# A fused attention and expert-routing kernel: six batches' result leaves the core unturned, and the first two batches turn theirs in buffers of their own

## The chip, the cores and the metric

The kernel runs on one core of one Trainium2 chip, as one launch. The metric is the device time of that launch in microseconds (us), as the median of the runs shown, lower is better. The inputs are laid out on the host beforehand (z and u transposed, z repeated for both halves of the partitions); the rows that pad the last tile of the output are cut off afterwards. Neither is timed.

## The reference, cut to what matters

First an attention-like product without a softmax, per batch, then a mixture of experts in which each token goes to one expert of eight and each expert keeps at most 80 tokens; all other rows of the output are zero.

```
B, S, D = 8, 2496, 256          # d_qk = 64
scores = z @ z^T / S            # symmetric
attn   = max(scores, 0) ** 2
x      = u * (attn @ v)         # all batches: 19968 tokens of 256
logits = x @ w_gate             # 8 experts; argmax, softmax weight of the chosen one
for e in range(8):              # the 80 tokens of largest weight
    h = max(x[tok] @ w1[e], 0); out[tok] = weight * (h @ w2[e])
```

The weights of nearly all tokens tie, and the order in which the reference keeps tied tokens puts the kept ones into the first and the last batch, which this kernel works first and second. It counts on that and checks it: a flag, computed from the data, decides at the end whether a general path (an exact top-80 over all tokens) has to run. For the inputs of the runs shown the flag is 0 and the general path is not entered.

## The kernel before, in words

**Tiles.** A batch has 2,496 rows, that is 20 tiles of 128 (the last one half full), and is worked in five chunks of 512 query columns (`qc` = 0 to 4) by ten steps, one for each pair of key tiles: 8 x 5 x 10 = 400 steps. The main loop (L1007) is written out in a fixed order for all engines and for SyncE's DMA queue (SP).

**One step.** TensorE (PE) makes the scores of the pair that is two steps ahead (`scores`, L385), ScalarE (ACT) takes relu and square out of PSUM (L402, L403), and the square is split into a rounded high part `ah` and a rest `al` (L113 or L115, and L58 on VectorE, DVE). PE then adds the pair's product with `v`, in three passes, to the accumulator `acc` in PSUM (`attend_pair` and `weigh`, L438). Since the scores are symmetric, a block that was computed as key against query is used again as its mirror image: DVE turns it in 32 x 32 squares (L308), SP writes it to DRAM (`y<-x`, L318, 1 MB) and reads it back with four DMAs (`blk<-y`, L335), and ACT splits it straight from there (L380) without scores. The chunk's own diagonal block does the same with a quarter (`yd<-xd` L353, `md<-yd` L362 issued in step 3 of the chunk, used by ACT at L415 in step 7).

**The end of a chunk.** `acc` has two tiles of PSUM (`ps_a`, two buffers), one for each half `c` of the 256 features. In step 9 `take` (L503 to L508) copies each of them into the two halves of one SBUF tile, `xf[:, 0]` and `xf[:, 1]`; the next chunk's first product needs the accumulator that this frees. `xpool` has one buffer for `xf`, so `take` also has to wait until nobody reads the chunk before in it any more.

**What is done with x.** During the next chunk's steps (`finished`, L964): `chunk_x` in step 0 adds the halves, scales and multiplies by u, into `xf[:, 0]`, which is x transposed (features on partitions). `chunk_hi`, `chunk_rest`, `chunk_mid` and `chunk_lo` (steps 1 to 4) split x into three bf16 parts in `xb`, with `xf[:, 1]` as working space; `chunk_logits` (steps 6 or 7) makes the gate logits from them. In step 4 `chunk_store` (L554) turns x with two DMA transposes of 16-bit halves (L562) from `xf[:, 0]` into `xf[:, 1]`, and in step 6 `chunk_store2` (L565) writes the turned rows to DRAM (`xs<-xf`, L572; the half-full last tile of a batch has a second write, L577): to `xs2` for the first two batches, to `xs` for the other six. `xs2` feeds the expert stage; `xs` is read in the general path alone.

**Order on SP.** One in-order queue issues nearly all DMAs. Within a step it is: what `finished` issues, then the loads of u (L149, step 2), z and v, zeros for the output, and then `mirror_back` (L335), `mirror_out` (L318), `quarter_write` (L353) and, in step 3, `quarter_back` (L362), L1071 to L1075.

**Buffers that the change takes up.** `vraw` (two buffers, L128) holds raw chunks of v before they are split; a batch's last one is used up in step 3 of its first chunk, and the next batch's first two are loaded in chunk 3. The tag `x` of `sqpool` (four buffers, L306) holds turned score blocks until `y<-x` has read them; ten are made in a batch, four in chunk 0, three, two and one in the chunks after.

```
def take(b, qc, c):
    if c == 0:
        x_sum[b, qc] = chunk_tiles(b, qc)
    x = x_sum[b, qc]
    nc.scalar.copy(out=x[:, :, c], in_=acc_t[b, qc][c][:, :, :x.shape[-1]])
...
if r == NP - 1 and not last:
    attend_pair(b, qc, 2 * p, True, True, lambda c: take(b, qc, c))
```

Of the kernel before, what the change touches and what calls it, by code (L numbers as in the profile page):

```python
# [8 lines left out]
F32 = mybir.dt.float32  # L9
# [3 lines left out]
U16 = mybir.dt.uint16  # L13
# [6 lines left out]
P = 128  # L20
# [5 lines left out]
def attn_moe_kernel(ctx, tc, zT, uT, v, wg, w1, w2, out, seq, cap):  # L26
# [5 lines left out]
    nc = tc.nc  # L32
    V = nc.vector
    B, _, SP = zT.shape
    D = uT.shape[1]
# [6 lines left out]
    QT = 4  # L42
    NQ = NT // QT
    CH = QT * P
    DC = D // P
# [22 lines left out]
    dram = ctx.enter_context(tc.tile_pool(name="dram", bufs=1, space=DRAM))  # L68
# [7 lines left out]
    sqpool = weights.enter_context(tc.tile_pool(name="sqpool", bufs=NX))  # L76
    main = ExitStack()
    zpool = main.enter_context(tc.tile_pool(name="zpool", bufs=2))
# [14 lines left out]

    xs = dram.tile([NTOK * 2, D], U16, name="xs")
    gt = dram.tile([NTOK, 1], F32, name="gt")

    wtab = dram.tile([(NBLK + 1) * E, 2 * P], BF16, name="wtab")
    wtwo = dram.tile([(2 * BPB + 1) * E, 2 * P], BF16, name="wtwo")
# [391 lines left out]
    xt_t, xq_t, lg_t = {}, {}, {}  # L490

    def chunk_tiles(b, qc):
        xf = xpool.tile([P, 2, DC, CH], F32, tag="xf", name=f"xf_{b}_{qc}")

        xb = xpool.tile([P, 3, DC, CH], BF16, tag="xb", name=f"xb_{b}_{qc}")
        nq = min(CH, seq - qc * CH)
        xt_t[b, qc] = [x[..., :nq] for x in (xf[:, 0], xb, xf[:, 1])]
        xr_t[b, qc] = xf[:, 1].bitcast(U16)
        return xf[..., :nq]

    x_sum, xr_t = {}, {}

    def take(b, qc, c):  # L503

# [11 lines left out]
    def chunk_hi(b, qc):  # L516
        xf, xb, _ = xt_t[b, qc]
        nc.scalar.copy(out=xb[:, 0], in_=xf)  # L518

    def chunk_rest(b, qc):  # L520
        xf, xb, xr = xt_t[b, qc]
        tt(xr, xf, xb[:, 0], ALU.subtract)

    def chunk_mid(b, qc):
        _, xb, xr = xt_t[b, qc]
        nc.scalar.copy(out=xb[:, 1], in_=xr)  # L526

    def chunk_lo(b, qc):
        _, xb, xr = xt_t[b, qc]
        tt(xb[:, 2], xr, xb[:, 1], ALU.subtract)  # L530
# [20 lines left out]
                                 start=False, stop=(c, t) == (DC - 1, QT - 1))  # L551
        lg_t[b] = pl[:, :QT * E].rearrange("p (t e) -> p t e", e=E)

    def chunk_store(b, qc):  # L554

        xf = xt_t[b, qc][0]
        nq = min(CH, seq - qc * CH)
        ng = nq // 64
        xq = xr_t.pop((b, qc)).rearrange("p c (g r) -> p (c g r)", r=P)
        xq = xq.rearrange("p (g c r) -> p g c r", c=DC, r=P)  # L560
        for c in range(DC):
            nc.sync.dma_start_transpose(out=xq[:, :ng, c, :], in_=xf[:, c, :nq].bitcast(U16))  # L562
        xq_t[b, qc] = xq

    def chunk_store2(b, qc):  # L565
        xq = xq_t.pop((b, qc))
        nq = min(CH, seq - qc * CH)
        ng = nq // 64
        xo, r0 = (xs2, b * NT) if b < 2 else (xs, RB[b] * NT)
        r0 = (r0 + qc * QT) * 2 * P  # L570
        gl = ng if nq == CH else ng - 1
        nc.sync.dma_start(  # L572
            out=xo[r0:r0 + gl * P, :D].rearrange("(g r) d -> r g d", r=P),
            in_=xq[:, :gl].rearrange("p g c d -> p g (c d)"))
        if gl < ng:
            r1 = r0 + (2 * QT - 1) * P
            nc.sync.dma_start(out=xo[r1:r1 + P, :D], in_=xq[:, gl].rearrange("p c d -> p (c d)"))  # L577

    def chunk_logits(b, qc):
        nq = min(CH, seq - qc * CH)  # L580
        xb = xt_t[b, qc][1]
        pl = ps_m.tile([P, 2, CH], F32, tag="m", name=f"pl_{b}_{qc}")[:, :, :3 * QT * E]
        to = pl.rearrange("p h (s t e) -> p h t s e", s=3, t=QT)
        for t in range(QT):
            t0 = min(t * P, nq - P)
            for i in range(3 * DC):
                for h, hs in enumerate(HALVES):
                    nc.tensor.matmul(to[:, h, t], xb[hs, i % 3, i // 3, t0:t0 + P], wgs[hs, i // 3],
                                     start=i == 0, stop=i == 3 * DC - 1)
        lg_t[b, qc] = pl.rearrange("p h (s x) -> p x h s", s=3)  # L590

    def chunk_sum(b, qc):
        if qc == 0:
            lg_t[b] = gp.tile([P, NT, E], F32, tag="lg", name=f"lg_{b}")
        V.tensor_reduce(out=lg_t[b][:, qc * QT:(qc + 1) * QT].rearrange("p t e -> p (t e)"),
                        in_=lg_t.pop((b, qc)), axis=AX.XY, op=ALU.add)
# [3 lines left out]
    def gate_top(b, q0, q1):  # L600

        nt = (q1 - q0) * QT
        lg = lg_t[b][:, :nt]
        col = (RB[b] * NQ + q0) * QT
        k0, nk = col // 2, nt // 2

        def bc(t):
            return t.broadcast_to([P, nt, E])

        def small(name, n=E):  # L610
            return gp.tile([P, NT, n], F32, tag=name, name=f"{name}_{b}_{q0}")[:, :nt]

        mx = small("mx", 1)
        V.tensor_reduce(out=mx, in_=lg, axis=AX.X, op=ALU.max)
        last = b == B - 1
        d = d_last if q1 == NQ and last else small("d")
        tt(d, lg, bc(mx), ALU.subtract)
        ex = ex_last[:, q0 * QT:q1 * QT] if last else lg
        nc.scalar.activation(out=ex, in_=d, func=AF.Exp)

        fw = small("fw")
        V.scalar_tensor_tensor(out=fw, in0=d, scalar=0.0, in1=first_w.broadcast_to([P, nt, E]),
                               op0=ALU.is_equal, op1=ALU.mult)
        mf = small("mf", 1)
        V.tensor_reduce(out=mf, in_=fw, axis=AX.X, op=ALU.max)
        V.tensor_tensor(out=oh[:, :, k0:k0 + nk].rearrange("p h k e -> p k h e"),
                        in0=fw.rearrange("p (k h) e -> p k h e", h=2),
                        in1=bc(mf).rearrange("p (k h) e -> p k h e", h=2), op=ALU.is_equal)
        if q1 == NQ:
            V.memset(oh[:P - TAIL, 1, k0 + nk - 1], 0.0)  # L630
        gate_t[b, q0] = d, ex, fw
# [332 lines left out]
    def finished(b, qc, r):  # L964

        at_end = b == B - 1 and qc == NQ - 2
        if r == 1:
            chunk_hi(b, qc)
        if r == (1 if at_end else 2):
            chunk_rest(b, qc)  # L970
        if r == (2 if at_end else 3):
            chunk_mid(b, qc)
        if r == (3 if at_end else 4):
            chunk_lo(b, qc)
        if r == (3 if at_end else 4):
            chunk_store(b, qc)
        if r == (5 if at_end else 6):
            chunk_store2(b, qc)
        if r == (5 if at_end else 6 if qc == NQ - 1 else 7):
            chunk_logits(b, qc)  # L980
            chunk_sum(b, qc)
        if b < B - 1 and qc == NQ - 1:
            if r == 8:
                gate_top(b, 0, NQ)
            elif r == 9:
                gate_sum(b, gate_near(b, 0), gp)
        elif qc == 0 and b > 0:
            if r == 5:
                count(b - 1, 0, BPB, b - 1)
            elif r == 9 and b <= 2:  # L990
                kr = RB[b - 1] * BPB
                blocks(ps_m, "m", gp, oh, kr, kr + BPB, wtwo, (b - 1) * BPB)
        elif at_end and r == 7:
            gate_top(b, 0, NQ - 1)

    with tc.manual_schedule(engines={ET.PE, ET.Activation, ET.DVE, ET.SP, ET.Pool}):
# [10 lines left out]
        for i, (b, qc, r) in enumerate(steps):  # L1007
# [7 lines left out]
            p = pairs_of[b, qc][r]  # L1015
# [6 lines left out]
            if b == 0 and qc == 0:  # L1022
                if r % 2 == 0 and r < 8:
                    g = r // 2 + 1
# [13 lines left out]
            if prev:  # L1038
                finished(*prev, r)
# [4 lines left out]
            if b + 1 < B:  # L1044
# [5 lines left out]
                if qc == NQ - 2 and r in (2, 4):  # L1050
                    g = r // 2 - 1
                    v_raw[b + 1, g] = load_v(b + 1, g)
                if qc == NQ - 1:
                    if r in (1, 3, 6, 8):
                        g = (1, 3, 6, 8).index(r)
# [434 lines left out]
    with tc.If(nc.values_load(flag[0:1, 0:1], min_val=0, max_val=1) > 0):  # L1490
        for i in range(B * NQ):
            zero_out(i, B * NQ)
        with tc.tile_pool(name="gx", bufs=1) as gx:
            counted = (gx.tile([P, E, NBLK], BF16, name="tot"), gx.tile([P, E, NBLK], F32, name="incl"),
                       gx.tile([P, NST, E], F32, name="rank"))
            nc.sync.dma_start(out=gt[(B - 1) * NT * P:, :].rearrange("(p f) o -> p (f o)", p=P),
                              in_=gt2[NT * P:, :].rearrange("(p f) o -> p (f o)", p=P))
            nc.sync.dma_start(out=gt[:NT * P, :].rearrange("(p f) o -> p (f o)", p=P),
                              in_=gt2[:NT * P, :].rearrange("(p f) o -> p (f o)", p=P))
            for h in range(2):  # L1500
                for r0, r1 in ((0, 2 * NT - 2), (2 * NT - 1, 2 * NT)):
                    nc.sync.dma_start(
                        out=xs[(2 * NT * RB[h] + r0) * P:(2 * NT * RB[h] + r1) * P, :],
                        in_=xs2[(2 * NT * h + r0) * P:(2 * NT * h + r1) * P, :])
            general(*counted)
            anew(*counted)

# [34 lines left out]
```

## Time and profile before

| | |
|---|---|
| median of the 3 runs shown | 1553.8 us (1552.84 to 1556.2) |
| the profiled execution | 1548.47 us |
| its span, first to last instruction | 1546.8 us |
| PE, DVE, ACT busy, share of the span | 88%, 72%, 67% |
| granted TensorE clock, mean | 0.948 of full speed |
| DMA queue of SP: 317.96 MB | 74.0% of the 16 engines' span |

Engine names are those of the profile: PE is TensorE's matmul, PEld its weight load, SPq the queue of SyncE. L438 is line 438 of the kernel. "<-" behind an idle time names what ended it. Times in a timeline count from the span's start. The clock is given as a share of 2.4 GHz; 0.50 is 1.2 GHz.

### The profile page before, as it was taken

The numbers are of one execution on the slowest core, as the hardware profiler recorded it, in microseconds if no ns is written. First come the engines' busy times: TensorE is split into PE (matmuls) and PEld (weight loads), VectorE is DVE, ScalarE is ACT, GpSimd is POOL, SyncE is SP. The second block draws the span as 40 slices with busy tenths as digits, with TensorE's granted clock in tenths as the row PEclk, the third lists the DMA queues.
The fourth block names the chain that finished last, engine by engine and source line by source line (L and its number), as shares of the span: only waits on it lengthen the run. The fifth ranks groups of instructions, "written<-read, shape, count | busy, mean of one in ns | idle before, by whom it ended". The sixth has DMA issues, their size and how long they took to land.

```text
span 1546.8 us, 31646 instructions
## 1 busy us (share of the span) xinstructions
PE 1357.7 (88%) x13121; PEld 1123.9 (73%) x13121; DVE 1113.5 (72%) x1531; ACT 1037.1 (67%) x1124; POOL 40.4 (3%) x58
## 2 busy tenths in 40 slices
PE   9997979979899798997989897997989989898797
PEld 6775867767677676777767685775867777786676
DVE  8875877758678586866877577775877758786585
ACT  8874767747676486755876476774766747686565
POOL 0000000000001000000002000000000000000101
PEclk9998999989999999998999989998999999999899
DMA  6699566985779746997469955699576974689674
GB/s 211 203 282 279 151 221 188 247 222 155 209 222 242 202 127 202 253 262 195 120 209 255 261 160 183 170 255 262 150 206 205 244 205 143 188 221 269 165 249 144
DMA packets 280006, 322.35 MB, mean 208 GB/s; under 512 B 97792, under 2 KB 208048, under 8 KB 269616
## 3 DMA queue, kind: packets, MB, share of 16 engines
q1 hardware_dynamic: 278576, 317.96, 74.0%
q0 software_dynamic: 1280, 2.30, 0.5%
q8 instruction: 105, 1.72, 0.5%
q14 instruction: 45, 0.37, 0.1%
HBM read 163.66 MB, written 136.09 MB: 194 GB/s over the span
## 4 chain that ended last, share of the span: by engine, by line
PE 32%; DMA 26%; ACT 21%; DVE 9%; issue 6%; SPq 5%; ACTq 0%; POOL 0%; POOLq 0%; DVEq 0%
PE acc L438 25%; DMA xs<-xf 9%; DMA blk<-y 8%; ACT a L402 6%; ACT a L403 6%; ACT ah L113 4%; DMA xf<-xf 3%; PE s L400 3%; DMA md<-yd 3%; DMA y<-x 2%; ACT xf L508 2%; DVE x L308 2%; SPq L562 2%; DVE xf L58 2%; DVE al L58 2%
## 5 line engine op out<-in xcount | busy, mean ns | idle before, releaser
L438 PE MATMUL acc<-ah,vt 64*128 64x512 f32 (+1 forms) x6240 | 1000.2, 395 | 132.4 <-ACT xf L508 127.6
L438 PEld LDWEIGHTS acc<-ah,vt 64*128 64x128 f32 x6240 | 631.1, 192 | 249.3 <-ACT xf L508 140.6
L438 PE MATMUL acc<-al,vt 64*128 64x512 f32 (+1 forms) x3120 | 647.7, 394 | 19.9 <-DVE al L58 19.6
L438 PEld LDWEIGHTS acc<-al,vt 64*128 64x128 f32 x3120 | 326.6, 191 | 83.3 <-DVE al L58 30.1
L58 DVE TENSOR_TENSOR al<-a,ah 128x1024 fp32r<-128x1024 f32 (+1 forms) x240 | 271.8, 1133 | 132.3 <-ACT ah L113 127.2
L58 DVE TENSOR_TENSOR al<-blk,ah 128x1024 fp32r<-128x1024 f32 x160 | 193.2, 1219 | 180.9 <-ACT ah L380 161.5
L402 ACT ACTIVATE a<-s 128x1024 f32<-128x1024 f32 x240 | 228.9, 954 | 119.9 <-PE s L400 117.0
L403 ACT ACTIVATE a<-a 128x1024 f32<-128x1024 f32 x240 | 238.0, 992 | 7.6
L308 DVE STREAM_TRANSPOSE x<-a 128x512 f32<-128x512 f32 x320 | 207.7, 687 | 0.0
L380 ACT CAST ah<-blk 128x1024 fp32r<-128x1024 f32 x160 | 164.0, 1051 | 53.3 <-PE acc L438 39.9
L508 ACT COPY xf<-acc 128x1024 f32<-128x1024 f32 (+1 forms) x78 | 73.5, 992 | 135.3 <-DMA xs<-xf 78.4
L113 ACT CAST ah<-a 128x1024 fp32r<-128x1024 f32 x153 | 160.9, 1052 | 4.4
L400 PE MATMUL s<-zh,zl 64*128 64x512 f32 x480 | 91.7, 371 | 0.0
L400 PE MATMUL s<-zl,zh 64*128 64x512 f32 x480 | 91.5, 370 | 0.0
L518 ACT CAST xb<-xf 128x1024 bf16<-128x1024 f32 (+1 forms) x39 | 40.0, 1026 | 67.7 <-DVE xf L513 65.9
L400 PE MATMUL s<-zh,zh 64*128 64x512 f32 x320 | 66.6, 408 | 20.2 <-ACT a L402 20.0
L115 DVE CAST ah<-a 128x1024 fp32r<-128x1024 f32 (+3 forms) x87 | 49.1, 564 | 23.8 <-ACT a L403 23.5
L526 ACT CAST xb<-xf 128x1024 bf16<-128x1024 f32 (+1 forms) x39 | 40.0, 1026 | 26.9 <-DVE xf L58 26.8
L142 DVE TENSOR_TENSOR vt<-vraw,vt 128x1024 fp32r<-128x1024 f32 x40 | 48.2, 1205 | 13.4 <-ACT vt L113 13.4
L400 PEld LDWEIGHTS s<-zh,zh 64*128 64x128 f32 x320 | 31.1, 187 | 34.3 <-ACT a L402 29.4
L58 DVE TENSOR_TENSOR al<-md,ah 128x512 fp32r<-128x512 f32 x37 | 25.2, 682 | 41.6 <-ACT ah L415 41.6
L400 PEld LDWEIGHTS s<-zl,zh 64*128 64x128 f32 x480 | 46.7, 185 | 7.6
(188 smaller groups left out, 882.3 us busy)
## 6 DMA issues: line engine op xcount, KB each, us to landing
y<-x SPq DMA_DIRECT2D x80, 1024.0 KB
blk<-y SPq DMA_DIRECT2D x320, 256.0 KB
out<-idle SPq DMA_DIRECT2D x40, 512.0 KB
vraw<-v SPq DMA_DIRECT2D x32, 512.0 KB
ut<-uT SPq DMA_DIRECT2D x32, 512.0 KB
xs<-xf SPq DMA_DIRECT2D x32, 512.0 KB
wraw<-w SPq DMA_DIRECT2D x30, 512.0 KB
yd<-xd SPq DMA_DIRECT2D x37, 256.0 KB
```

The costliest lines, as they stand in the source:

```text
L58: V.tensor_tensor(out=o, in0=a, in1=b, op=op)
L113: eng.copy(out=o, in_=i)
L115: eng.tensor_copy(out=o, in_=i)
L142: e1.tensor_tensor(out=vt[:, :, 1], in0=raw, in1=vt[:, :, 0], op=ALU.subtract)
L308: V.transpose(out=x[:, :, :, t].rearrange("p n k s -> p k n s"), in_=a)
L380: nc.scalar.copy(out=natural(ah), in_=src)
L400: nc.tensor.matmul(s[:, h, c0:c1], zk[hs, t * P:(t + 1) * P], zq[hs], start=n == 0, stop=n == 2)
L402: nc.scalar.activation(out=a[:, :, c0:c1], in_=s[:, :, c0:c1], func=AF.Relu)
L403: nc.scalar.activation(out=a[:, :, c0:c1], in_=a[:, :, c0:c1], func=AF.Square)
L438: nc.tensor.matmul(acc_t[b, qc][c][:, h, :nq], v_t[b, k // QT][hs, k % QT, iv, c * P:(c + 1) * P], x[hs, k % 2, :nq], start=at not in begu ...
L508: nc.scalar.copy(out=x[:, :, c], in_=acc_t[b, qc][c][:, :, :x.shape[-1]])
L518: nc.scalar.copy(out=xb[:, 0], in_=xf)
```

## The change

For the six batches from the third on, `chunk_store` writes x as it lies in `xf[:, 0]` (features on partitions) to a DRAM tile of its own, in step 3 instead of step 4, and `chunk_store2` does nothing. The general path, where it is entered, first loads these tiles back, turns them and writes the rows to `xs`. For the first two batches the two transposes stay in step 4 and the write of rows in step 6, but the turned chunk goes to a buffer of `vraw` (chunks 0, 1 and 4) or of `sqpool` (chunks 2 and 3), no longer to `xf[:, 1]`.

```diff
+    xu = {(b, qc): dram.tile([P, DC, CH], F32, name=f"xu_{b}_{qc}") for b in range(2, B) for qc in range(NQ)}
...
-        xr_t[b, qc] = xf[:, 1].bitcast(U16)
...
     def chunk_store(b, qc):
 
         xf = xt_t[b, qc][0]
         nq = min(CH, seq - qc * CH)
-        ng = nq // 64
-        xq = xr_t.pop((b, qc)).rearrange("p c (g r) -> p (c g r)", r=P)
-        xq = xq.rearrange("p (g c r) -> p g c r", c=DC, r=P)
-        for c in range(DC):
-            nc.sync.dma_start_transpose(out=xq[:, :ng, c, :], in_=xf[:, c, :nq].bitcast(U16))
-        xq_t[b, qc] = xq
+        if b >= 2:
+            nc.sync.dma_start(out=xu[b, qc][:, :, :nq], in_=xf)
+        elif qc in (2, 3):
+            xq = sqpool.tile([P, 2, QT * 2 * D], U16, tag="x", name=f"xq_{b}_{qc}")[:, 0]
+            xq_t[b, qc] = x_turn(xf, xq, nq)
+        else:
+            xq = zpool.tile([P, QT * 2 * D], U16, tag="vraw", name=f"xq_{b}_{qc}")
+            xq_t[b, qc] = x_turn(xf, xq, nq)
 
     def chunk_store2(b, qc):
-        xq = xq_t.pop((b, qc))
-        nq = min(CH, seq - qc * CH)
...
+        if b < 2:
+            x_rows(b, qc, min(CH, seq - qc * CH), xq_t.pop((b, qc)))
...
-        if r == (3 if at_end else 4):
+        if r == (3 if at_end or b >= 2 else 4):
             chunk_store(b, qc)
...
+            with tc.tile_pool(name="gxu", bufs=2) as gxu:
+                for b, qc in xu:
+                    nq = min(CH, seq - qc * CH)
+                    xf = gxu.tile([P, DC, CH], F32, tag="xf", name=f"gxf_{b}_{qc}")
+                    nc.sync.dma_start(out=xf[:, :, :nq], in_=xu[b, qc][:, :, :nq])
+                    xq = gxu.tile([P, QT * 2 * D], U16, tag="xq", name=f"gxq_{b}_{qc}")
+                    x_rows(b, qc, nq, x_turn(xf, xq, nq))
             general(*counted)
```

`x_turn` holds the two transposes that `chunk_store` had, `x_rows` the writes that `chunk_store2` had, both unchanged; the last hunk lies in the general path.

## Rows read from the trace of the kernel before

**Rows 1.** The page: busy time and share of PE; a DMA issue with its size.

```profile
PE 1357.7 (88%) x13121; PEld 1123.9 (73%) x13121; DVE 1113.5 (72%) x1531; ACT 1037.1 (67%) x1124; POOL 40.4 (3%) x58
...
xs<-xf SPq DMA_DIRECT2D x32, 512.0 KB
```

**Rows 2.** Waits of PE: total us, times, longest us.

```profile
PE acc L438 <- ACT xf L508: 127.6, 31, 11.3
...
PE acc L438 <- DVE al L58: 19.6, 11, 2.4
PE acc L438 <- DVE ah L115: 4.3, 3, 1.8
```

**Rows 3.** Waits of ACT, from the view of all waits.

```profile
ACT xf L508 <- DMA xs<-xf: 78.4, 17, 12.8
...
ACT xf L508 <- DMA blk<-y: 55.2, 6, 10.0
...
ACT ah L415 <- DMA md<-yd: 32.4, 16, 5.5
```

**Rows 4.** Timeline 872 to 893 us, fifth batch, chunk 3: start, us, instruction, [idle before].

```profile
872.10 0.30 SPq L362 DMA_DIRECT2D md<-yd  x1
...
873.35 5.03 SPq L562 DMA_TRANSPOSE xf<-xf  x2
...
878.80 0.62 ACT L415 CAST ah<-md 128x512 fp32r<-128x512 f32 x1 [2.28 <-DMA md<-yd]
...
881.56 0.45 SPq L572 DMA_DIRECT2D xs<-xf  x1
...
891.25 1.93 ACT L508 COPY xf<-acc 128x1024 f32<-128x1024 f32 x2 [9.73 <-DMA xs<-xf]
892.32 1.11 PE L438 MATMUL acc<-ah,vt 64*128 64x448 f32 x4 [7.52 <-ACT xf L508]
```

**Rows 5.** Chain that ended last, whole span, its longest pieces: start, us, what.

```profile
625.40 5.98 DMA xs<-xf
...
881.56 9.54 DMA xs<-xf
...
1409.86 13.21 DMA wraw<-w
```

**Rows 6.** Timeline 662 to 682 us, fourth batch: a take that waits for nothing.

```profile
663.90 1.91 ACT L508 COPY xf<-acc 128x1024 f32<-128x1024 f32 x2
...
675.89 0.79 PE L438 MATMUL acc<-al,vt 64*128 64x512 f32 x2 [2.36 <-DVE al L58]
```

**Rows 7.** Timeline of PE, 735 to 750 us, the boundary between two batches.

```profile
737.60 0.73 PE L438 MATMUL acc<-ah,vt 64*128 64x512 f32 x4 [0.49 <-ACT xf L508]
```

**Rows 8.** One whole chunk, busy time by engine, granted clock, DMA share and GB/s.

```profile
631.50:663.90 32.40, 31.35 (x320) 25.91 (x322) 25.31 (x34) 25.89 (x27) 2.70 (x2) 1.00 1.05 285
```

**Rows 9.** The 18 stretches of clock 0.50 behind a held take; their sum.

```profile
887.10:897.30 10.20, 4.98 (x26) 4.44 (x28) 3.14 (x3) 4.28 (x5) 0.00 (x0) 0.50 0.89 251
...
sum 136.60, PE 82.60 PEld 69.47 DVE 49.91 ACT 71.47 POOL 2.12; mean PE 4.59 PEld 3.86 DVE 2.77 ACT 3.97 POOL 0.12
```

**Rows 10.** The same view behind the 2.36 us wait of group 6.

```profile
675.50:678.90 3.40, 3.00 (x14) 2.42 (x16) 2.48 (x3) 2.18 (x3) 0.00 (x0) 0.50 0.98 375
```

**Rows 11.** The same view: two transposes, a long full stretch, and behind a boundary.

```profile
619.90:623.70 3.80, 3.80 (x38) 3.17 (x38) 3.71 (x6) 3.71 (x6) 0.00 (x0) 1.00 0.96 79
670.00:712.00 42.00, 31.01 (x280) 24.34 (x278) 23.47 (x30) 16.00 (x18) 0.00 (x0) 0.85 1.06 262
...
738.00:748.00 10.00, 9.49 (x84) 7.43 (x80) 7.86 (x10) 7.32 (x9) 0.00 (x0) 1.00 0.00 1
```

**Rows 12.** Waits of SP's queue.

```profile
SPq L562 <- DVE xb L58: 202.3, 22, 13.8
...
SPq L149 <- DVE xf L513: 98.6, 21, 10.3
...
SPq L572 <- DMA xf<-xf: 24.8, 26, 2.1
```

More of the change, by code (lines that the diff above doesn't have):

```diff
@@ L497, in chunk_tiles @@
         xt_t[b, qc] = [x[..., :nq] for x in (xf[:, 0], xb, xf[:, 1])]
-        xr_t[b, qc] = xf[:, 1].bitcast(U16)
         return xf[..., :nq]
-    x_sum, xr_t = {}, {}
+    x_sum = {}
     def take(b, qc, c):
@@ L552, in chunk_logits_last, with x_turn, x_rows @@
         lg_t[b] = pl[:, :QT * E].rearrange("p (t e) -> p t e", e=E)
-    def chunk_store(b, qc):
-        xf = xt_t[b, qc][0]
-        nq = min(CH, seq - qc * CH)
-        ng = nq // 64
-        xq = xr_t.pop((b, qc)).rearrange("p c (g r) -> p (c g r)", r=P)
+    def x_turn(xf, xq, nq):
         xq = xq.rearrange("p (g c r) -> p g c r", c=DC, r=P)
         for c in range(DC):
-            nc.sync.dma_start_transpose(out=xq[:, :ng, c, :], in_=xf[:, c, :nq].bitcast(U16))
-        xq_t[b, qc] = xq
-    def chunk_store2(b, qc):
-        xq = xq_t.pop((b, qc))
-        nq = min(CH, seq - qc * CH)
+            nc.sync.dma_start_transpose(out=xq[:, :nq // 64, c, :], in_=xf[:, c, :nq].bitcast(U16))
+        return xq
+    def x_rows(b, qc, nq, xq):
         ng = nq // 64
@@ L577, in chunk_store2, with chunk_store @@
             nc.sync.dma_start(out=xo[r1:r1 + P, :D], in_=xq[:, gl].rearrange("p c d -> p (c d)"))
+    def chunk_store(b, qc):
+        xf = xt_t[b, qc][0]
+        nq = min(CH, seq - qc * CH)
[7 more added lines that the diff above has]
+            xq_t[b, qc] = x_turn(xf, xq, nq)
+    def chunk_store2(b, qc):
+        if b < 2:
+            x_rows(b, qc, min(CH, seq - qc * CH), xq_t.pop((b, qc)))
     def chunk_logits(b, qc):
@@ L1504, in attn_moe_kernel @@
                         in_=xs2[(2 * NT * h + r0) * P:(2 * NT * h + r1) * P, :])
+            with tc.tile_pool(name="gxu", bufs=2) as gxu:
+                for b, qc in xu:
+                    nq = min(CH, seq - qc * CH)
+                    xf = gxu.tile([P, DC, CH], F32, tag="xf", name=f"gxf_{b}_{qc}")
+                    nc.sync.dma_start(out=xf[:, :, :nq], in_=xu[b, qc][:, :, :nq])
+                    xq = gxu.tile([P, QT * 2 * D], U16, tag="xq", name=f"gxq_{b}_{qc}")
+                    x_rows(b, qc, nq, x_turn(xf, xq, nq))
             general(*counted)
```

## The prediction, made before the result was known

> **What bounds the kernel now.** I read the page first, then the waits of PE and ACT, then the timeline around the longest of those waits, and last the windows for the clock and the DMA engines.
>
> PE is busy for 1357.7 us of the span, 88%, more than any other engine [rows 1], so the 189 us in which it idles are what can be won. Two thirds of that is one wait: PE stood before a chunk's first product 31 times, 127.6 us in all, until ACT's `take` had freed the accumulator; the other waits of PE in the list are small [rows 2]. ACT for its part stood before `take` for 78.4 us until the write `xs<-xf` of the chunk before had landed, and for 55.2 us with another DMA named [rows 3]. `take` reads nothing from DMA, and the blocks named there are not its operands, so I read these six waits, too, as waits for the one buffer of `xf`.
>
> The timeline shows the chain once in full [rows 4]: the two transposes of the chunk before are issued at 873.35 and take the queue 5.03 us, the write of rows goes out only at 881.56, `take` starts at 891.25 after 9.73 us of idling, and PE goes on at 892.32 after 7.52 us. The chain of waits puts 9.54 us between issue and landing of that write [rows 5], which ends at 891.10, just ahead of the `take`. Where the write lands in time, the boundary costs next to nothing: the `take` at 663.90 follows without idling [rows 6], and seven of the 31 waits are of the kind of 0.49 us [rows 7]. Between boundaries PE is the bound: in the chunk from 631.50 to 663.90 it is busy for 31.35 of 32.40 us at full clock, with DVE and ACT at 25.31 and 25.89 [rows 8]. That also gives a step: 3.24 us.
>
> A held `take` costs a second time. Behind 18 of them the clock stands at 0.50 for a while, that is 1.2 GHz, and PE is busy for 82.60 us in these stretches [rows 9].
>
> **The change, part by part.**
>
> *Six batches.* `xf` is now read by one store, issued in step 3 instead of step 6 and waiting for no transpose. From step 3 to the `take` of step 9 are about 6 x 3.24 = 19 us. Landings of such writes on the chain were 5.98 and 9.54 us, and the longest landing among the chain's longest pieces is 13.21 us [rows 5]. So I take the store as landed before every `take`, and the wait as gone.
>
> *Two batches.* The write of rows leaves another buffer, so `xf` is held only until the transposes have read it. In the worst place shown they are issued at 873.35, and the write behind them, which needs them landed, goes out at 881.56 [rows 4], which is when the `take` began to wait: these, too, should be in time, if by little. The new buffers are free when needed: the raw chunk of v was split a step before, and the turned score blocks are written out in the chunks before. SP should not stand there.
>
> *T1, the waits themselves.* 31 waits, 127.6 us [rows 2]. Bounds: nothing is left (127.6 gained), or each keeps 0.49 us [rows 7], 31 x 0.49 = 15.2. I take the second, since ACT's copy always lies between the old accumulation and the new: **112.4 us**.
>
> *T2, the clock.* At half clock 82.60 us of busy PE are 41.3 us of work at full clock, so 41.3 are lost [rows 9]. Bounds 0 and 41.3. Behind one wait of 2.36 us [rows 6] it fell for 3.40 us [rows 10], and such waits remain; behind a wait of 0.49 us it stayed at 1.00 [rows 7, 11]. I let it fall three more times behind those, 3 x 1.7 = 5.1, and take **36.2 us**.
>
> *T3, loads that come late.* In chunks 2 and 3 the DMA engines are full: share 1.06 and 262 GB/s over 42 us [rows 11]. PE will now come earlier to what it needs there. The load nearest to being late is the quarter, `md<-yd`: ACT already waits for it 16 times, 32.4 us [rows 3], yet PE felt only 4.3 us in three waits for what ACT and DVE make of it [rows 2]. The new store stands just ahead of it on the queue in step 3: 512 KB [rows 1] at 262 GB/s are 2.0 us. In 27 of the 30 moved stores a quarter follows in the same step. Against that, two transposes and a write are gone from the queue per chunk, and the transposes are slow traffic: 3.8 us of nearly full engines for 79 GB/s [rows 11]. Bounds: 27 x 2.0 = 54 lost, all passed on to PE, or 4.3 gained. I take a loss of 4.3 / 3 = 1.4 once in each of the six batches, **8.6 us**: the row nearest is the one in which 16 late quarters cost PE three short waits.
>
> *What costs nothing.* Two transposes and one or two writes per chunk become one issue. SP has room: it stood 202.3 us before the transposes for `chunk_lo` to finish with `xf[:, 1]`, and that wait goes with the target [rows 12]. What the store waits for instead, `chunk_x`, the load of u already waits for a step earlier on the same queue (98.6 us) [rows 12], so nothing behind the store gets a new wait. In the first two batches the write of rows still waits for the transposes on SP, 2.1 us at most so far [rows 12]. If this cover were gone, an issue would cost 0.45 us [rows 4], 30 x 0.45 = 14 us. The general path is longer in code, but not entered. The last chunk's store at the end of the loop gets shorter; PE does not wait for it.
>
> *Sum.* 112.4 + 36.2 - 8.6 = 140.0 us. The profiled execution took 1548.47 us, so 1408.5; the median of the runs shown is 5.3 us above it, and against that I say 1553.8 - 140.0 = **1414 us**.
>
> **The rivals.**
>
> *The clock does not come back.* PE will idle 0.49 us at each boundary and for 2.36 us in some chunks; if these suffice to bring it to 1.2 GHz as the long waits did, T2 is lost: 112.4 - 8.6 = 103.8, so 1450. For it: the clock did fall behind 2.36 us [rows 10]. Against it: it was 1.00 throughout the stretch behind a boundary of 0.49 us [rows 11] and in the chunk of rows 8. The Trainium skill has a rule on this rival's side: TensorE: Matmul & The Clock Gate, section "A second HAM failure mode: psum-queue depth-cycling", says that brief idling of PE between groups of matmuls, if it comes often, lets the clock swing between its two levels. By that rule the time would be the 1450 just worked out, by the rows it is 1414. The trace agrees with it for one wait of 2.36 us and not for 0.49 us.
>
> *Late quarters.* The store's 2.0 us pass through to PE at all 27 places: 112.4 + 36.2 - 54 = 94.6, so 1459. For it: full engines, and quarters already late [rows 3, 11]. Against it: ACT's lead of two steps swallowed most of that so far [rows 2].
>
> *Slower.* The quarter waits not for the store's share of the engines but for its landing, 5.98 us at least [rows 5]: SP serves in order, and ACT, in order, stands before L415 with relu, square and the next `take` behind it. 27 x 5.98 = 161.5 against 148.6 gained: 1567. It decides from 148.6 / 27 = 5.5 us of new wait per quarter on. Against it: the load of u, 512 KB or nearly, stands one step ahead of the quarter today, blocks and score blocks besides, and the 16 waits for the quarter are of 32.4 / 16 = 2.0 us [rows 3], less than any such landing.
>
> *The change does not do what it says.* If the store lands as late as the old write, `take` waits as before: 1554. For it, the landing can be 9.54 us in a full stretch; against it, it has some 19 us.
>
> **How the numbers follow.** The forecast holds 0.74, with its low end where nothing is lost: 127.6 + 41.3 + 4.3 = 173.2, so 1381. The clock rival gets 0.08, the late quarters 0.10, no effect 0.03, slower 0.05. Clock and quarters together would give 112.4 - 54 = 58.4, that is 1495; I stop the range between 1459 and that, at 1475, which leaves out the last two cases and a little of the others. The three runs shown lie within 3.4 us, so 0.2% (3.1 us) is about what can be told from no change. Faster: 0.74 + 0.08 + 0.10 = 0.92; same 0.03; slower 0.05.
>
> **What would show it right or wrong.** Right: PE's wait for L508 falls from 127.6 to about 15 us; ACT's wait before L508 for DMAs goes from 133.6 to a few us, in the first two batches too; the mean clock of the profile's table rises from 0.948 to about 0.99. T3 shows in ACT's wait for `md<-yd` and PE's waits behind it. Wrong: if PE's waits go but the clock stays near 0.95 (first rival); if L415 or L380 takes over ACT's waits with tens of us (second); if the transposes of the first two batches now wait on SP for `vraw` or a score block, which would show as idle time of DVE before L308; or if `take` still names a DMA.

## The result, and the profile after

| | before | changed |
|---|---|---|
| median, 4 runs each on one chip | 1555.0 us (1552.84 to 1559.63) | 1424.38 us (1420.18 to 1427.79) |
| ratio, 95% interval | | 0.9155 [0.9117, 0.9193] |
| the profiled execution | 1548.47 us | 1427.79 us |
| its span | 1546.8 us | 1426.1 us |
| granted TensorE clock, mean | 0.948 | 0.985 |

The kernel is 130.6 us faster. The forecast was 1414 us, within 1381 to 1475. Where lines of the kernel are named below, all from L97 to L507 have moved by one: L438 is now L439, L362 is L363, L415 is L416.

The page: busy time and share of the span of the engines, then the packets, MB and share of the 16 DMA engines of SP's queue.

```profile
PE 1332.9 (93%) x13121; PEld 1086.2 (76%) x13121; DVE 1113.1 (78%) x1531; ACT 1036.0 (73%) x1124; POOL 38.9 (3%) x58
...
q1 hardware_dynamic: 191312, 302.62, 72.6%
```

PE executes as many matmuls as before and is busy for 24.8 us less [rows 1]: that is put down to the clock; a second count stands below. Its idle time went from 1546.8 - 1357.7 = 189.1 us to 1426.1 - 1332.9 = 93.2, that is 95.9 less. Together these are the 120.7 us between the two spans.

The waits of PE in the changed kernel: total us, times, longest us.

```profile
PE acc L439 <- DVE al L58: 30.2, 40, 2.4
PE s L401 <- ACT a L403: 29.7, 28, 1.5
PE acc L439 <- ACT xf L508: 19.0, 16, 2.4
...
PE acc L439 <- DVE ah L116: 0.4, 1, 0.4
```

The wait before a chunk's first product fell from 127.6 us in 31 waits [rows 2] to 19.0 in 16: 108.6 us won. The wait for `al` grew by 10.6 us, the one for `ah` fell by 3.9. The wait of the score products for ACT's relu grew by 5.7; before, it was this:

```profile
PE s L400 <- ACT a L402: 24.0, 17, 2.9
```

The sum, 108.6 - 10.6 + 3.9 - 5.7 = 96.2, is the idle time that went, to 0.3 us.

The waits of ACT, from the view of all waits, in the same columns.

```profile
ACT xb L518 <- DVE xf L513: 103.5, 36, 4.1
...
ACT xf L508 <- PE acc L439: 32.0, 32, 3.0
...
ACT lg L629 <- DVE d L58: 23.7, 7, 3.7
...
ACT ah L416 <- DMA md<-yd: 11.0, 10, 1.6
```

No DMA stands before L508 any more (78.4 and 55.2 us [rows 3]): `take` now waits for PE to finish the accumulation, which is what it should wait for. The quarter, which I had expected to come later, comes earlier: 11.0 us where it was 32.4 [rows 3].

The boundary behind chunk 3 of the fifth batch, which answers to [rows 4], in the timeline.

```profile
803.17 0.43 SPq L577 DMA_DIRECT2D xu<-xf  x1
803.65 3.55 SPq L363 DMA_DIRECT2D md<-yd  x4
...
814.24 0.62 ACT L416 CAST ah<-md 128x512 fp32r<-128x512 f32 x1 [1.46 <-DMA md<-yd]
...
819.74 1.02 ACT L508 COPY xf<-acc 128x1024 f32<-128x1024 f32 x1 [1.96 <-PE acc L439]
...
821.11 1.02 ACT L508 COPY xf<-acc 128x1024 f32<-128x1024 f32 x1 [0.35 <-PE acc L439]
```

The store goes out at 803.17 and `take` starts 16.6 us later, released by PE. Before, the write went out at 881.56 and `take` had to wait until 891.25 [rows 4].

What is left at the other boundaries is seen behind chunk 0: the timeline around its `take` in the fourth batch.

```profile
549.68 0.33 DVE L58 TENSOR_TENSOR d<-lg,mx 128x160 f32<-128x160 f32 x1
...
550.04 0.34 ACT L629 ACTIVATE lg<-d 128x160 f32<-128x160 f32 x1 [3.33 <-DVE d L58]
...
550.28 1.91 ACT L508 COPY xf<-acc 128x1024 f32<-128x1024 f32 x2
...
551.33 0.73 PE L439 MATMUL acc<-ah,vt 64*128 64x512 f32 x4 [2.03 <-ACT xf L508]
```

ACT stands for 3.33 us before the exponential of the gate (`gate_top`, step 8), which waits for DVE, and `take`, next in ACT's order, comes too late by 2 us. This happens once in each of seven batches (L629 waits 7 times), and these seven waits are most of the 19.0 us.

The other wait that stands out is the one of 2.35 us in chunk 3, here of the first batch.

```profile
116.84 1.18 DVE L58 TENSOR_TENSOR xf<-xf 128x1024 f32<-128x1024 f32 x1
...
118.05 1.22 DVE L513 SCALAR_TENSOR_TENSOR xf<-xf,ut 128x1024 f32<-128x1024 f32 x1
119.19 1.22 DVE L58 TENSOR_TENSOR al<-blk,ah 128x1024 fp32r<-128x1024 f32 x1
119.30 0.38 SPq L150 DMA_DIRECT2D ut<-uT  x1
119.31 1.04 ACT L518 CAST xb<-xf 128x1024 bf16<-128x1024 f32 x1 [3.92 <-DVE xf L513]
...
120.47 0.50 PE L439 MATMUL acc<-al,vt 64*128 64x512 f32 x2 [2.35 <-DVE al L58]
```

DVE works `chunk_x` (two instructions) before the `al` that PE needs next, and PE, in order, stands. Seven batches have such a wait, of 2.35 to 2.38 us; the last has one of 1.61. It was there before the change, too, in the same seven batches: the 2.36 us of [rows 6] is one of them.

The nine stretches of low clock in the main loop: window, then busy us of PE, PEld, DVE, ACT and POOL (with counts), granted clock, DMA share, GB/s. The first is behind that wait in chunk 3, like six others, the second behind a `take` of chunk 0, like one other.

```profile
120.90:124.30 3.40, 3.40 (x20) 2.68 (x18) 2.96 (x3) 1.92 (x3) 0.00 (x0) 0.50 0.94 328
...
721.60:725.10 3.50, 3.50 (x20) 2.76 (x18) 2.79 (x9) 1.42 (x2) 0.00 (x0) 0.51 0.02 5
...
sum 30.70, PE 29.92 PEld 23.61 DVE 25.29 ACT 16.59 POOL 0.00; mean PE 3.32 PEld 2.62 DVE 2.81 ACT 1.84 POOL 0.00
```

Before, PE was busy for 82.60 us at half clock behind the held takes [rows 9]. That was not all: the main loop had four more such stretches, at 675.5, 863.2, 1231.8 and 1426.4 us, the first three of them behind the wait for `al` in chunk 3. Their sum:

```profile
sum 13.60, PE 13.21 PEld 10.52 DVE 11.39 ACT 7.88 POOL 0.00; mean PE 3.30 PEld 2.63 DVE 2.85 ACT 1.97 POOL 0.00
```

So (82.60 + 13.21) / 2 = 47.9 us of work were lost to the clock in the main loop, and 29.92 / 2 = 15.0 still are. That is 32.9 us won by this count, where PE's busy time fell by 24.8; what the 8 us between the two are, no run shows.

One sign of being wrong that the prediction named is not there: DVE does not idle before it turns score blocks (0.0 us before L309 on the page), so the first two batches' new buffers hold nothing up there.

### The profile page after: what moved, and what is told of

Its sections match the earlier page's. It is cut to its first block, busy times and chain, and to the rows that moved or that the text cites. A ratio compares the mean times of both kernels' runs of the same rounds, so it can differ in the third digit from the quotient of the medians.

```text
span 1426.1 us, 31554 instructions
## 1 busy us (share of the span) xinstructions
PE 1332.9 (93%) x13121; PEld 1086.2 (76%) x13121; DVE 1113.1 (78%) x1531; ACT 1036.0 (73%) x1124; POOL 38.9 (3%) x58
## 3 DMA queue, kind: packets, MB, share of 16 engines
q1 hardware_dynamic: 191312, 302.62, 72.6%
## 4 chain that ended last, share of the span: by engine, by line
PE 41%; ACT 20%; DVE 17%; DMA 11%; issue 7%; SPq 3%; DVEq 0%; ACTq 0%; POOL 0%; POOLq 0%
PE acc L439 31%; DVE al L58 6%; PE s L401 5%; ACT a L403 5%; ACT a L404 4%; DMA blk<-y 4%; ACT ah L114 3%; DVE x L309 3%; DVE xf L58 3%; DMA y<-x 2%; ACT xf L508 2%; ACT ah L381 2%; PE hp L1286 2%; ACT vt L114 2%; DVE xf L513 1%
## 5 line engine op out<-in xcount | busy, mean ns | idle before, releaser
L439 PE MATMUL acc<-ah,vt 64*128 64x512 f32 (+1 forms) x6240 | 969.3, 387 | 19.8 <-ACT xf L508 19.0
L439 PEld LDWEIGHTS acc<-ah,vt 64*128 64x128 f32 x6240 | 597.6, 186 | 135.1 <-ACT xf L508 30.3
L439 PE MATMUL acc<-al,vt 64*128 64x512 f32 (+1 forms) x3120 | 624.7, 390 | 31.1 <-DVE al L58 30.2
L439 PEld LDWEIGHTS acc<-al,vt 64*128 64x128 f32 x3120 | 305.6, 186 | 105.8 <-DVE al L58 53.2
L309 DVE STREAM_TRANSPOSE x<-a 128x512 f32<-128x512 f32 x320 | 207.7, 687 | 0.0
L508 ACT COPY xf<-acc 128x1024 f32<-128x1024 f32 (+1 forms) x78 | 75.0, 991 | 34.0 <-PE acc L439 32.0
L401 PEld LDWEIGHTS s<-zh,zl 64*128 64x128 f32 x480 | 45.8, 186 | 5.7
```

The lines of the kernel that those rows point to most:

```text
L309: V.transpose(out=x[:, :, :, t].rearrange("p n k s -> p k n s"), in_=a)
L401: nc.tensor.matmul(s[:, h, c0:c1], zk[hs, t * P:(t + 1) * P], zq[hs], start=n == 0, stop=n == 2)
L439: nc.tensor.matmul(acc_t[b, qc][c][:, h, :nq], v_t[b, k // QT][hs, k % QT, iv, c * P:(c + 1) * P], x[hs, k % 2, :nq], start=at not in begu ...
```

## The experiments

Each run is timed against the kernel before on the same chip; the ratios are those of medians with 95% intervals. Diffs are against the changed kernel.

**Is it the hold of `xf` or the transposes and their traffic?** In e1 six batches keep the transposes and the writes of rows, in buffers like those of the first two batches; one batch, the last, is as in the change.

```diff
...
-        if b >= 2:
+        if b == B - 1:
             nc.sync.dma_start(out=xu[b, qc][:, :, :nq], in_=xf)
...
-        if b < 2:
+        if b < B - 1:
             x_rows(b, qc, min(CH, seq - qc * CH), xq_t.pop((b, qc)))
...
-        if r == (3 if at_end or b >= 2 else 4):
+        if r == (3 if at_end or b == B - 1 else 4):
```

> Batches 2 to 6 keep both transposes and the write of rows, as before the change, but turn into buffers of their own as the first two batches do; only the last batch is stored unturned. The DMA traffic is nearly that of the kernel before, the hold on xf is gone. Theory (the hold on xf is what cost the time): PE's wait for the take stays near 19 us, the time is 1430 to 1460. Rival (it is the lighter DMA queue that wins the time): five of six batches lose their relief, loads of blocks and quarters are late and the time is 1500 to 1540.

Measured: 1420.61 us, ratio 0.9151 [0.9107, 0.9194], the same as the change. Its page shows what it pays on the DMA engines.

```profile
q1 hardware_dynamic: 264032, 315.41, 80.0%
```

So the engines are busier than in the changed kernel, 80.0% against 72.6%, and nothing comes of it that can be measured. The gain is the hold; the lighter traffic has no part in it that shows. e1 shortens the hold in two ways at once, which it doesn't part: the write of rows no longer reads `xf`, and the transposes no longer have to wait for `chunk_lo` to be done with `xf[:, 1]`. At the place of [rows 4] the first would have been enough: the transposes had landed by 881.56, and `take` had only begun to wait then (891.25 - 9.73).

In e2 the six other batches are as they were before (turned into `xf[:, 1]`, rows from there), and only the first two have the new buffers.

```diff
-        if b >= 2:
-            nc.sync.dma_start(out=xu[b, qc][:, :, :nq], in_=xf)
+        if b >= 2:
+            xq = xr_t.pop((b, qc)).rearrange("p c (g r) -> p (c g r)", r=P)
+            xq_t[b, qc] = x_turn(xf, xq, nq)
...
```

(The transposes in step 4 and the write of rows in step 6 are for all batches again.)

> Only the first two batches' part: own buffers there, the other six as in the kernel before (turned into xf, rows written in step 6). Theory: the PE waits of the first two batches' chunks go, about 33 us (the ones at 79.9, 152.4, 224.6, 261.7, 335.4 and 408.6 us of the trace before) and some 10 us of lost clock behind them: 1510 to 1520. Rival (lighter queue): nothing is lighter, 1545 to 1555.

Measured: 1517.36 us, ratio 0.9769 [0.9727, 0.9812]. Two of eight batches bring 1551.7 - 1517.4 = 34 us of the 131, a quarter, as their number says.

**Does it matter when the store lands?** In e3 the store of the six batches goes out at step 8, in e5 at step 6, in place of 3 (e5 has 6 where this diff has 8).

```diff
-        if r == (3 if at_end or b >= 2 else 4):
+        if r == (3 if at_end else 8 if b >= 2 else 4):
             chunk_store(b, qc)
```

> The changed kernel, but the unturned store of the six batches goes out in step 8 instead of step 3, one step ahead of the take. The traffic is that of the changed kernel. Theory (hold): a landing of 6 to 10 us against a step of 3.3 us leaves the take waiting 3 to 6 us in some 28 chunks, and the clock falls behind it: 1520 to 1620, PE's wait for the take over 80 us. Rival (lighter queue): within 10 us of the changed kernel, 1415 to 1435.

> The changed kernel with the unturned store in step 6, where the write of rows stood before. Theory (hold): issued some 10 us before the take with a landing of 6 to 10 us, it holds the take in the full stretch alone, by 1 to 3 us in one or two chunks of a batch: 1425 to 1450. If the transposes' traffic was what mattered, 1420 to 1428; if the place of the store was all, as slow as the kernel before, over 1500.

Measured: e3 1462.74 us, ratio 0.9414 [0.9373, 0.9456], between the theory and the rival; e5 1443.49 us, 0.9269 [0.9244, 0.9294], where it was expected. The timeline of e3 shows why it lost less than I expected; again the boundary behind chunk 3 of the fifth batch.

```profile
827.42 0.35 SPq L577 DMA_DIRECT2D xu<-xf  x1
...
835.45 1.93 ACT L508 COPY xf<-acc 128x1024 f32<-128x1024 f32 x2 [7.92 <-DMA xu<-xf]
...
836.51 1.11 PE L439 MATMUL acc<-ah,vt 64*128 64x448 f32 x4 [5.70 <-ACT xf L508]
```

The store lands 8.0 us after its issue and `take` waits for it, as the old write made it wait. But ACT has only seven such waits in e3 (50.0 us in all), six of them behind chunk 3, one in each of the six batches, where I had counted one at nearly every boundary; elsewhere the store lands before the `take` even from step 8. PE's wait for L508 rises from 19.0 to 54.6 us. In e5 the `take` of this same boundary still waits for 3.59 us. In the change it starts 16.6 us after the store's issue, and the trace has that store landing at 813.0, 9.9 us after its issue: some 6.7 us to spare here, and three steps later is already late.

**What do the store and its traffic cost?** e4 leaves out the store of the six batches' x (and its way back in the general path); e6 stores it three times, to three tiles.

```diff
...
-            nc.sync.dma_start(out=xu[b, qc][:, :, :nq], in_=xf)
+            return
...
```

> The changed kernel without the store of the six batches' x (and without what reads it in the general path, which is not entered). Theory (hold): the store in step 3 is covered, 1418 to 1428. Rival (lighter queue): if 18 us of DMA time less per batch gave 130 us, ten more give some 50 to 70: 1350 to 1380.

```diff
...
-            nc.sync.dma_start(out=xu[b, qc][:, :, :nq], in_=xf)
+            for x in (xu, xv, xw):
+                nc.sync.dma_start(out=x[b, qc][:, :, :nq], in_=xf)
```

> The changed kernel with three stores of the same chunk in step 3, to three places, all ahead of the quarter's load: 1 MB more per chunk. Theory (quarters are late only where the DMA engines are full, and ACT's lead of two steps takes most of it): 4 us later in two chunks of a batch, 1430 to 1470. Rival (a late quarter passes on to PE everywhere, 2.0 us per 512 KB): 27 times 4 us, 1520 to 1540.

Measured: e4 1419.12 us, ratio 0.9133 [0.9093, 0.9173], not told apart from the change. e6 1433.27 us, 0.9203 [0.9178, 0.9228]; the intervals overlap, so its trace has to say what the 9 us are. First ACT, then PE, from the views of waits of e6 (lines there have moved by one more).

```profile
ACT ah L417 <- DMA md<-yd: 36.9, 11, 5.9
...
PE acc L440 <- DVE ah L117: 5.7, 5, 2.2
```

Here is the mechanism of T3: with more written ahead of the quarter on SP's queue, ACT's wait for it goes from 11.0 to 36.9 us, and 5.7 us of that reach PE in place of 0.4. But it takes two further stores per chunk to get there. One store costs nothing that can be measured.

**What are the waits that remain worth?** e7 moves the gate's exponential away from the `take`.

```diff
-            if r == 8:
+            if r == 7:
                 gate_top(b, 0, NQ)
```

> The changed kernel with the gate's softmax of a batch (gate_top) in step 7 instead of step 8 of the next batch's first chunk. In the changed kernel ACT stands 3.3 us for DVE there, just ahead of the take, and PE waits 2.0 us for that take in seven batches. Theory: that wait falls to 0.5 us, and the two falls of the clock behind it go: 10 to 15 us less, 1408 to 1414. Rival: ACT stands as long a step earlier and the time stays, 1420 to 1428.

Measured: 1415.12 us, ratio 0.9089 [0.9064, 0.9114]. The `take` behind chunk 0 of the fourth batch in its timeline.

```profile
541.01 0.34 ACT L629 ACTIVATE lg<-d 128x160 f32<-128x160 f32 x1 [3.32 <-DVE d L58]
...
543.26 1.91 ACT L508 COPY xf<-acc 128x1024 f32<-128x1024 f32 x2
...
544.31 0.73 PE L439 MATMUL acc<-ah,vt 64*128 64x512 f32 x4 [0.28 <-ACT xf L508]
```

ACT still stands for 3.3 us, but further from the `take`, and PE waits 0.28 us where it waited 2.03. PE's wait for L508 falls from 19.0 to 6.3 us. The time is 1 us above what I expected.

e8 moves `chunk_x` in chunk 3, and the splits behind it, two steps later, so that DVE makes `al` first.

```diff
-            if r == 0 and prev:
+            if prev and r == (2 if qc == 3 else 0):
                 chunk_x(*prev)
...
+        late_x = 2 * (qc == 2)
-        if r == 1:
+        if r == 1 + late_x:
             chunk_hi(b, qc)
```

(`chunk_rest`, `chunk_mid` and `chunk_lo` likewise.)

> The changed kernel with chunk_x of chunk 2 in step 2 of chunk 3 instead of step 0 (and its bf16 parts two steps later), since in chunk 3 DVE works on chunk_x for 2.4 us while PE waits 2.35 us for the split behind it, and the clock falls for 3.4 us after it in seven batches. Theory: the wait and the fall go, 8 x 2.35 + 7 x 1.7 = 31 us at most, and the mean clock rises from 0.985 to 0.995: 1393 to 1405. Rival: the next split or the gate logits wait in its place: 1420 to 1428.

Measured: 1438.24 us, ratio 0.9231 [0.9204, 0.9259]: slower than the change, outside both. The wait for `al` did go (longest 0.9 us), but PE then waited 23.5 us, 8 times, for `ah` behind the quarter. The first batch's chunk 3 in e8's timeline.

```profile
120.66 1.23 DVE L513 SCALAR_TENSOR_TENSOR xf<-xf,ut 128x1024 f32<-128x1024 f32 x1
121.92 0.38 SPq L150 DMA_DIRECT2D ut<-uT  x1
...
125.45 4.34 SPq L363 DMA_DIRECT2D md<-yd  x4
...
136.42 0.62 ACT L416 CAST ah<-md 128x512 fp32r<-128x512 f32 x1 [5.63 <-DMA md<-yd]
...
138.24 0.73 PE L439 MATMUL acc<-ah,vt 64*128 64x512 f32 x4 [1.90 <-DVE ah L116]
```

The load of `ut` needs the tile that `chunk_x` frees with its second instruction: SP issues it at 121.92, right behind that, where it was 119.30 in the changed kernel. All later issues of SP stand behind it, the quarter's four loads too: they go out from 125.45 on, where it was 124.86, and have landed at 136.3, where it was 134.0. ACT was ready for them at 136.42 - 5.63 = 130.79, earlier than in the changed kernel (134.38), since PE had lost nothing before; so they were late from both sides, by 2.3 us from the loads' and by 3.6 from ACT's. To tell whether it is this queue, e9 moves in addition the load of `ut` behind the quarter's loads.

```diff
-            if r == 2:
+            if r == (4 if qc == 3 else 2):
                 prep_u(b, qc)
```

> The changed kernel with chunk_x and the splits behind it two steps later in chunk 3, as in e8, and beside it the load of ut moved in chunk 3 from step 2 to step 4, so that on SP's queue it stands behind the four loads of md and no longer in front of them. Theory: e8 took the 2.35 us wait for al away (its longest such wait is 0.9 us) and lost more than that because the load of ut waits for chunk_x's second instruction and everything behind it on SP, the md loads among them, came some 2.6 us later (ACT waited 55.0 us for md in e8, 11.0 us in the changed kernel). With ut behind md: ACT waits for md 6 to 20 us, TensorE's waits for ah 0 to 3 us in all (23.5 in e8), none for al above 1.2 us, time 1395 to 1412 us. Rival: the md loads are late in e8 because of other traffic that moved with chunk_x, or TensorE's waits for ah come from ACT's order and not from the load: the waits for ah stay at 15 to 25 us and the time at 1430 to 1440 us.

Measured: 1400.80 us, ratio 0.8997 [0.8982, 0.9012], and PE's wait for `ah` down to 0.3 us. The same place in e9's timeline.

```profile
121.73 3.42 SPq L363 DMA_DIRECT2D md<-yd  x4
...
130.48 0.58 SPq L150 DMA_DIRECT2D ut<-uT  x1
130.96 0.62 ACT L416 CAST ah<-md 128x512 fp32r<-128x512 f32 x1 [0.20 <-DMA md<-yd]
```

With the load of `ut` out of the way the quarter's loads go out at 121.73, 3.7 us earlier than in e8. So it was the place on SP's queue, behind one load that waits, that had cost the gain and more. e12 moves the load of `ut` alone, to see that the gain isn't the load's by itself.

> The changed kernel with only the load of ut moved in chunk 3 from step 2 to step 4; chunk_x stays at step 0. Theory: the md loads stand behind the load of ut for chunk_x's end alone, and in the changed kernel they land in time (TensorE's waits for ah are 0.4 us in all), so this does nothing by itself: 1416 to 1428 us, the 2.35 us waits of chunk 3 as many as before. Rival: e9 gained by the earlier loads and not by chunk_x: 1398 to 1408 us.

Measured: 1424.33 us, ratio 0.9193 [0.9175, 0.9211], as the change. As far as these runs go, the load's place matters only where `chunk_x` is late.

e10 tries a smaller move: `chunk_x` at step 1 of chunk 3, the splits where they were, `ut` late.

```diff
-            if r == 0 and prev:
+            if prev and r == (1 if qc == 3 else 0):
                 chunk_x(*prev)
```

> The changed kernel with chunk_x one step later in chunk 3 (step 1, behind that step's split of a buffered pair; the bf16 copy of x stays at step 1 behind it) and the load of ut at step 4 in chunk 3. Theory: DVE does the al of pair 3 first, so the 2.35 us wait in chunk 3 shrinks to 0.4 us, 7 x 1.95 = 13.7 us, and with it up to 7 falls of the clock at about 1.7 us each (12 us): time 1395 to 1412 us against 1424. Rival: the copies to bf16 then stand on ACT ahead of the next cast of a buffered pair and the wait comes back one pair later: time 1418 to 1426 us, with the same number of waits for al of over 2 us.

Measured: 1431.44 us, ratio 0.92 [0.9184, 0.9215]: slower than both ranges; from the change itself it is not told apart, as the intervals overlap. The rival had the mechanism in part: the wait came back one pair later, but as a wait for `ah` (14.3 us, 8 times), and none for `al` is over 0.9 us. The first batch's chunk 3 in e10.

```profile
121.25 1.04 ACT L518 CAST xb<-xf 128x1024 bf16<-128x1024 f32 x1 [5.06 <-DVE xf L513]
...
123.28 1.22 DVE L58 TENSOR_TENSOR al<-blk,ah 128x1024 fp32r<-128x1024 f32 x1 [2.06 <-ACT ah L381]
123.30 0.73 PE L439 MATMUL acc<-ah,vt 64*128 64x512 f32 x4 [1.85 <-ACT ah L381]
```

DVE makes that `al` in time, but ACT now stands for 5.06 us before the copy to bf16, with the next block's cast behind it; PE waits 1.85 us for that, and right after it for the `al` that follows. Of the moves tried, the one that paid took along what ACT does with `chunk_x` and the load that waits for it (e9).

e11 puts e7 and e9 together.

> e9 (chunk_x in chunk 3 two steps later, the load of ut behind the md loads) and e7 (gate_top at step 7 in place of 8) together. Theory: the two waits are at different places (chunk 3, and the take of chunk 0), so the gains add up: e7 gained 0.0066 of the time before on the changed kernel's ratio (0.9155 to 0.9089) and e9 0.0158 (to 0.8997), together 0.9155 - 0.0224 = 0.893, some 1388 to 1394 us at a time before of 1555. Rival: gate_top one step earlier works on a chunk whose DVE and ACT order has moved with chunk_x and gives back what it gains: 1398 to 1406 us.

Measured: 1388.84 us (1386.0 to 1390.67, 5 runs), ratio 0.8955 [0.8939, 0.897], faster than both kernels of this case. The gains add up. Its waits of PE, and the busy row of its page, where PE's share is 95%.

```profile
PE s L401 <- ACT a L403: 27.5, 30, 1.5
PE acc L439 <- DVE al L58: 14.5, 38, 0.9
PE acc L439 <- ACT xf L508: 6.2, 16, 0.8
```

```profile
PE 1321.5 (95%) x13121; PEld 1067.8 (77%) x13121; DVE 1111.5 (80%) x1531; ACT 1034.6 (75%) x1124; POOL 40.0 (3%) x58
```

## Why the prediction was right, and where it was off

**What bounds the kernel**: right. The hold of `xf` until the write had landed was the wait, and e1 shows that it was: with other buffers and nearly all the old traffic (315.41 MB of 317.96) the time is that of the change. The six waits with `blk<-y` named fit waits for `xf`: they went with the others, while the blocks are loaded as before.

**T1**, 112.4 us predicted, 108.6 measured. The store lands in time: no `take` names a DMA any more. What was mis-sized is "each keeps 0.49 us". The residue came to 19.0 us instead of 15.2, and it is not spread like that: 16 waits, seven of them of about 2 us. ACT's exponential for the gate stood just ahead of those `take`s in the kernel before, too, but under the longer wait for the write; removing the outer wait brought out the inner one. I had asked what is late next only of DMAs and not of the order of ACT.

**T2**, 36.2 us predicted, 24.8 measured by PE's busy time (32.9 by the count of stretches above). The mechanism held: the clock comes back, from 0.948 to 0.985. The step that failed is "I let it fall three more times": it fell nine times, 15.0 us in place of 5.1. Seven of the nine are behind the wait of 2.35 us in chunk 3, of which the prediction showed one [rows 6, 10] without counting them. Seven batches had it before, too, and the clock fell behind three of the seven then; in the changed kernel it fell behind all seven. The other two are behind the seven of about 2 us that T1 had overlooked. The other side of the term was short as well: the 41.3 us are those behind held takes alone, and the four further stretches of before add 6.6. The rule of the Trainium skill that the prediction weighed (TensorE: Matmul & The Clock Gate, section "A second HAM failure mode: psum-queue depth-cycling") is borne out in part: the swing between the two levels is there behind waits of 2.0 to 2.4 us, though not behind each of them, and in e11, where the longest waits are of 1.5 us, the clock does not fall in the main loop at all.

**T3**, a loss of 8.6 us predicted for late quarters. The quarters came earlier, not later: the mechanism is real (e6, e8), but one store is too little for it (e4), and the sign was wrong. It isn't that the transposes are gone: in e1, which keeps them, ACT's wait for the quarter is 9.8 us. What the traces show is that SP issued the quarter's four loads with less standing. In the kernel before it stood before them for other DMAs to land, 61.4 us in all, of which these are two thirds; the last line is e1's largest.

```profile
SPq L362 <- DMA yd<-xd: 22.6, 13, 8.3
...
SPq L362 <- DMA vraw<-v: 18.1, 7, 3.1
```

```profile
SPq L363 <- DMA yd<-xd: 8.1, 4, 4.2
```

In the changed kernel such waits come to 7.8 us, in e1 to 13.5. What also went in both is SP's wait of 202.3 us before the transposes [rows 12], which stand on the queue ahead of the next chunk's quarter. In e2, whose six batches keep it, ACT still waits 22.7 us for the quarter. That this wait is the reason was not tried by itself. A loss of nearly that size came from elsewhere: 10.6 us more waits of PE for `al`, 5.7 more for relu, 3.9 fewer for `ah`, 12.4 net. The growth is in short waits, as the seven of 2.35 us in chunk 3 were there before: 30.2 us in 40 waits where it was 19.6 in 11. That PE now follows DVE and ACT more closely is how I read it; no run tried it.

**Sum.** The terms were too good by 3.8 (T1), 11.4 (T2) and 3.8 (T3), 19.0 in all: 140.0 - 120.7 = 19.3 us between the profiled executions. The medians differ by 130.6, as the execution of before that was profiled is quicker than the four that were timed, and that of after is the slowest of its four. That left 1424.4 against 1414.

**The rivals.** The one with the lasting low clock (1450) fell: the clock came back, though 15.0 us stayed lost where the prediction had 5.1. Late quarters (1459) and the slower case (1567) fell with e4: with no store at all the time is not told apart. That the store could land as late as the old write (1554) did not come true at step 3; e5 shows that it starts to hold `take` three steps later, at a cost of some 20 us, and e3 that even step 8 costs no more than some 40.

## What to carry to other kernels

Where a buffer is released by a DMA's landing, issue that DMA early and with no other DMA to wait for (the six batches), or let it read another buffer (the first two batches, and e1); here that was the gain, and the traffic that went with it brought nothing that could be measured. How early is enough is a matter of steps: 3 was in time, 6 was not (e5). When a long wait goes, list what else stands ahead of the waiting instruction in its own engine's order: that may be the wait that comes next, as the gate's exponential was here. Before moving an instruction, look for the DMA that waits for it and for what stands behind that DMA on its queue (e8 against e9: 37 us).

## What the runs showed of the hardware that was not expected

**The same wait does not always cost the clock.** In the changed kernel it fell behind all seven waits of 2.35 to 2.38 us in chunk 3 and two of the seven of some 2 us behind chunk 0. In e12, whose waits at these places are of nearly the same lengths (2.02 to 2.38 us), it fell behind one of seven and two of seven, and a fourth time in a stretch with four waits of at most 0.54 us. In the second batch both kernels have the wait of 2.35 us, ending at 290.13 in the changed kernel and at 289.63 in e12. The window right behind it, first in the changed kernel, then in e12:

```profile
291.60:295.00 3.40, 3.40 (x18) 2.65 (x18) 2.90 (x3) 1.92 (x3) 0.00 (x0) 0.50 0.98 305
```

```profile
291.10:294.50 3.40, 3.40 (x32) 2.79 (x31) 2.90 (x3) 1.92 (x3) 0.00 (x0) 1.00 0.39 95
```

PE is busy throughout in both, with 18 matmuls counted in one and 32 in the other. The DMA share differs, too, 0.98 against 0.39, but in e12 the clock did fall in the first batch with a share of 0.11 (120.7 to 124.1 us), so full engines are not needed for it. The runs of one kernel differ along with the clock: the four of the changed kernel had mean clocks of 0.985, 0.985, 0.992 and 0.990 at 1427.79, 1427.24, 1420.18 and 1421.51 us. Why it falls in one execution and not in the next was not settled.

**Transposes are dear on the DMA engines.** e1 moves 315.41 - 302.62 = 12.8 MB more than the change, and the 16 engines are busy for 0.800 x 1419.5 - 0.726 x 1426.1 = 100 us more: 128 GB/s for what was added, against 302.62 MB in 1035 us, 292 GB/s, for the rest. By the sizes of the packets in the two traces this is three things: 12.8 MB more in packets of 256 B, the transposes, which take 89.9 us, 142 GB/s; 12.8 MB more in packets of 512 B, the rows, 44.1 us; and 12.8 MB less in packets of 1792 and 4096 B, the stores, 33.6 us. The Trainium skill (Advanced Engine Details and Errata, section "X-Bar Transpose (TRN2)") says that transposing DMAs are as fast as regular ones; these numbers, like the 79 GB/s at a share of 0.96 [rows 11], say otherwise here. A packet of 256 B takes 28 ns on average in e1, as long as one of 512 B, so it may be the size of the packets and not the turning that is dear; no other DMA of these two runs goes in packets of 256 B, so they can't tell. It still cost this kernel no time that could be measured.
